# The first batch cut at token 256: four chunks of attention, two MLP units, then the rest, in program order and closed by a fence

## Chip, cores, metric

One core of a Trainium2 chip. The metric is device time in microseconds (us), the median of several executions. All runs quoted were in the same (fast) state. "PE" is TensorE, "DVE" VectorE, "ACT" ScalarE, "POOL" GpSimd, "SP" the engine that issues most DMAs. L-numbers are lines of the kernel that a profile belongs to, so they shift a little from kernel to kernel.

## The reference

```python
# q, k, v: (8 batches, 8 heads, 576 tokens, 64) float32
scores = q @ k.T / 8
ret = scores * where(i >= j, gamma[h] ** (i - j), 0)
attn = ret @ v                                    # (8, 8, 576, 64)
x = attn.transpose(0, 2, 1, 3).reshape(4608, 512)
h = x @ w_in                                      # (512, 2048), float32
g = max(h, 0) + alpha * min(h, 0)                 # alpha per column of h
out = g @ w_out                                   # (4608, 512)
```

## The kernel before

Attention runs by **pairs of heads** (4 pairs per batch, 32 in all) and by **chunks** of 64 tokens (9 per batch): transposes of k and q (`pt`), scores inside chunks (`ps`), states k^T v of chunks (`pu`), their running sums (`su`, copied into `sums`), and values (`pv`), which make x. The MLP runs by **blocks** of 256 tokens (`kb`) and **units** of 2 x 128 columns of h (`i`, 8 per block): 16 matmuls into `ph`, evictions to `g` (ScalarE and VectorE read the finished sums out of `ph`, and only then is `ph` free again), then products `po` with w_out, one unit later. The first two blocks use plain matmuls, the other sixteen a Strassen form (fewer multiplications, more additions). Block 1 needs tokens 256 to 511, block 2 the last 64 tokens of batch 0 and some of batch 1.

The weights come as 32 **pieces** of 512 KB, and each has to be converted.

```python
AHEAD = 5
def fetch(n):                                # SyncE: needs a landing buffer that is free
    ...
        t = free.pop(0)
        nc.sync.dma_start(raw, src)
def load_piece():
    ...
    nc.scalar.activation(a, hi.bitcast(FP32), ACTF.Abs)                    # "wa"
    nc.scalar.activation(lo, lo.bitcast(UINT32), ACTF.Copy, scale=2.0**-29) # "raw" or "w_in"
    nc.vector.tensor_scalar(c.bitcast(FP32), a, HI_MIN, HI_MAX, ALU.max, ALU.min)   # "wc"
    nc.vector.tensor_scalar(c, c, 3, 0x3FFFFFF8, ALU.logical_shift_left, ALU.bitwise_and)
    nc.vector.scalar_tensor_tensor(out=dst, in0=hi, scalar=-0x40000000, in1=c, ...)
    nc.gpsimd.tensor_tensor(out=dst, in0=dst, in1=lo, op=ALU.add)
    free.append(t)                           # the landing buffer is free after GpSimd's add
def load_weights(n):
    for _ in range(n):
        load_piece()
        fetch(npiece[1] + AHEAD)
```

The landing buffers are idle parts of other tiles. The loop that is cut by the change, shortened:

```python
for n in range(1, 4):
    loaded[n] = load_pair(n)                 # q, k, v of a pair, all 576 tokens
    fetch(2 * n)
PIECES = (2, 2, 2, 2, 8, 8, 8, 0)            # pieces converted beside pair n
UNITS = (0, 0, 0, 0, 4, 4, 4, 4)             # plain units beside pair n
for n, (b, c) in enumerate(pairs):
    if 3 < n + 1 < len(pairs):
        loaded[n + 1] = load_pair(n + 1)
    ...
    kT, qT = transposes(n);  load_weights(parts[3])
    at = scores(n, kT, qT);  pop_units(cuts[0]);  load_weights(parts[2])
    states(n, kn, vn);       pop_units(cuts[1]);  load_weights(parts[1])
    values(n, vn, qT, at);   pop_units(cuts[2]);  load_weights(parts[0])
    if c == NPAIR - 1:
        enqueue(b)                           # the first MLP units come after pair 3
```

Nothing fixes the order of instructions of different steps here: the layout of each engine's instruction stream is left to the scheduler.

## Time and profile before

| | before |
|---|---|
| time | 1077.85 us (1076.21 to 1079.26, 4 runs) |
| TensorE busy | 98% of a span of 1076.6 us |
| granted clock, mean | 0.993 |
| first MLP unit runs through | from 66 us |
| last weight piece enters VectorE | 122 us |

Between 80 and 120 us, weights, plain units and pairs 4 to 6 share the engines. Busy time by stretch of the kernel before (columns: PE, PEld, DVE, ACT, POOL busy with counts, granted clock, DMA share, GB/s):

```profile
80.00:90.00 10.00, 10.00 (x75) 7.00 (x68) 9.41 (x15) 5.87 (x16) 9.84 (x10) 1.00 0.85 224
90.00:100.00 10.00, 10.00 (x74) 7.03 (x75) 9.44 (x17) 6.37 (x12) 9.84 (x12) 1.00 0.60 201
100.00:110.00 10.00, 7.72 (x54) 4.89 (x53) 6.08 (x10) 6.13 (x11) 7.26 (x8) 0.93 0.90 280
110.00:120.00 10.00, 10.00 (x94) 6.90 (x93) 9.65 (x19) 7.16 (x17) 6.85 (x8) 0.90 0.61 131
```

Outside 100 to 110 us VectorE is busy 94 to 97% of the time, and TensorE stands still only once, for 2.3 us ahead of 107.6 us.

### The profile page before, as it was taken

How to read it: one execution, taken by the hardware profiler on the slowest of the kernel's cores; microseconds unless marked ns; L12 is line 12 of the kernel's file. 1: busy time of each engine (PE TensorE's matmuls, PEld its weight loads, DVE VectorE, ACT ScalarE, POOL GpSimd, SP SyncE). 2: the span in 40 equal slices, each digit the busy share in tenths (PEclk: the TensorE clock that was granted, in tenths of full speed). 3: DMA queues.
4: the chain of work that ended last, by engine and by line, in shares of the span. 5: the costliest groups of instructions: out<-in, count | busy, mean ns of one | idle time of the engine just before them, and what ended most of it. 6: DMA issues, size and time to landing. Idle time of an engine off the chain costs nothing.

```text
span 1076.6 us, 25072 instructions
## 1 busy us (share of the span) xinstructions
PE 1054.3 (98%) x10321; PEld 927.9 (86%) x10321; DVE 747.0 (69%) x1958; ACT 191.1 (18%) x549; POOL 217.4 (20%) x260
## 2 busy tenths in 40 slices
PE   6899999999999999999999999999999999999998
PEld 5666666899999999999999999999999999999997
DVE  5688612678687777786777777786768676667575
ACT  3666422211110111110100111111111110000000
POOL 4368743411020102010102110201011000100000
PEclk9989999999999999999999999999999999999999
DMA  8857413212222222211112222122222100000000
GB/s 199 242 155 231 100 25 63 76 36 64 45 65 43 56 46 52 47 43 34 35 43 40 60 46 65 35 65 46 65 46 54 24 21 1 21 1 21 1 21 20
DMA packets 212050, 63.25 MB, mean 59 GB/s; under 512 B 201168, under 2 KB 201184, under 8 KB 211936
## 3 DMA queue, kind: packets, MB, share of 16 engines
q1 hardware_dynamic: 209504, 61.04, 24.2%
q8 instruction: 82, 1.34, 0.5%
q10 hardware_dynamic: 2432, 0.60, 0.3%
q14 instruction: 32, 0.26, 0.1%
HBM read 52.17 MB, written 9.44 MB: 57 GB/s over the span
## 4 chain that ended last, share of the span: by engine, by line
PE 93%; DVE 2%; DMA 2%; ACT 1%; issue 1%; POOL 0%; SPq 0%; ACTq 0%; DVEq 0%
PE ph L392 38%; PE po L314 36%; PE ph L350 5%; PE po L329 4%; PE pv L565 3%; PE pv L560 2%; PE ps L523 2%; PE pu L538 2%; PE pt L494 1%; DMA raw<-in_moe_w_in_dram 1%; DMA w_in<-in_moe_w_in_dram 1%; DVE wc L245 1%; DVE wc L248 0%; DMA a<-in_moe_alpha_dram 0%; DMA kn<-in_k_dram 0%
## 5 line engine op out<-in xcount | busy, mean ns | idle before, releaser
L314 PE MATMUL po<-w_out,g 128*128 128x256 f32 x1792 | 407.8, 379 | 0.0
L314 PEld LDWEIGHTS po<-w_out,g 128*128 128x128 f32 x1792 | 330.8, 190 | 39.7
L403 DVE TENSOR_TENSOR g<-ph,g 128x256 f32<-128x256 f32 (+1 forms) x512 | 187.4, 387 | 180.2 <-PE ph L392 103.6
L392 PE MATMUL ph<-xb,w_in 128*128 128x128 f32 x2048 | 277.7, 279 | 0.0
L392 PEld LDWEIGHTS ph<-xb,w_in 128*128 128x128 f32 x2048 | 253.1, 192 | 8.2 <-issue 0.5
L392 PE MATMUL ph<-xt,w_in 128*128 128x128 f32 x1536 | 213.3, 275 | 0.0
L392 PEld LDWEIGHTS ph<-xt,w_in 128*128 128x128 f32 x1536 | 192.1, 192 | 0.0
L414 DVE TENSOR_TENSOR g<-g 128x128 f32<-128x128 f32 x512 | 144.0, 322 | 7.8
L398 ACT COPY g<-ph 128x128 f32<-128x128 f32 x128 | 34.0, 265 | 479.5 <-PE ph L392 472.0
L462 POOL TENSOR_TENSOR vn<-vn,th 128x512 f32<-128x512 f32 (+1 forms) x60 | 42.0, 718 | 380.9 <-DMA vn<-in_v_dram 380.8
L408 DVE SCALAR_TENSOR_TENSOR g<-g 128x512 f32<-128x512 f32 x128 | 94.3, 737 | 3.9
L406 DVE TENSOR_SCALAR g<-g,alpha 128x256 f32<-128x256 f32 x256 | 88.7, 388 | 4.5
L350 PE MATMUL ph<-xb,w_in 128*128 128x256 f32 x256 | 65.3, 404 | 2.8 <-DVE g L359 2.3
L375 POOL TENSOR_TENSOR xt<-xb,xt 128x256 f32<-128x256 f32 x32 | 25.1, 786 | 175.2 <-ACT xb L451 174.6
L350 PEld LDWEIGHTS ph<-xb,w_in 128*128 128x128 f32 x256 | 48.9, 198 | 13.2 <-issue 4.7
L329 PE MATMUL po<-w_out,g 128*128 128x512 f32 x128 | 57.8, 593 | 1.1 <-DVE g L359 1.1
L451 ACT COPY xb<-pv 128x128 f32<-128x128 f32 (+1 forms) x176 | 29.6, 269 | 129.1 <-PE pv L565 129.1
L329 PEld LDWEIGHTS po<-w_out,g 128*128 128x128 f32 x128 | 24.2, 190 | 24.5 <-issue 22.0
L552 ACT COPY sums<-su 64x512 f32<-64x512 f32 x64 | 39.5, 617 | 29.4 <-DVE su L549 28.6
L527 DVE SCALAR_TENSOR_TENSOR at<-ps,th,mask 128x320 f32<-128x320 f32 x64 | 32.4, 544 | 15.9 <-PE ps L523 15.9
L506 DVE STREAM_TRANSPOSE qT<-qn 128x576 f32<-128x576 f32 x24 | 18.7, 778 | 33.8 <-PE pv L565 30.5
L565 PE MATMUL pv<-qT,sums 128*64 128x64 f32 x1024 | 41.2, 235 | 0.2 <-ACT sums L552 0.2
(90 smaller groups left out, 686.8 us busy)
## 6 DMA issues: line engine op xcount, KB each, us to landing
out_dram<-osb SPq DMA_DIRECT2D x36, 256.0 KB, 2.3
kn<-in_k_dram SPq DMA_DIRECT2D x60, 128.0 KB, 2.9
vn<-in_v_dram SPq DMA_DIRECT2D x60, 128.0 KB, 2.7
kx<-in_k_dram SPq DMA_DIRECT2D x96, 72.0 KB, 2.4
qn<-in_q_dram SPq DMA_DIRECT2D x96, 72.0 KB, 2.5
raw<-in_moe_w_in_dram SPq DMA_DIRECT2D x11, 512.0 KB, 4.3
raw<-in_moe_w_out_dram SPq DMA_DIRECT2D x11, 512.0 KB, 4.6
w_in<-in_moe_w_in_dram SPq DMA_DIRECT2D x5, 512.0 KB, 6.0
```

What stands on the lines that cost most here:

```text
L314: nc.tensor.matmul(acc[kb][n // 2][:, n % 2, :], g[:, x, :], w_out[i][:, y, :], start=(i == 0 and n % 2 == 0), stop=(i == NU - 1 and (n % ...
L329: nc.tensor.matmul(acc[kb][m], g[:, 2 * x + m], w_out[i][:, 2 * x:2 * x + 2].rearrange("p x f -> p (x f)"), start=(i == 0 and x == 0), sto ...
L350: nc.tensor.matmul(ph[:, x], w_in[i // UST][:, cc // 2 * 2 + x, cc % 2, f0:f0 + P], xb[kb][:, cc], start=(cc == 0), stop=(cc == NCC - 1))
L392: nc.tensor.matmul(ph[m][:, o], w_in[i // UST][:, l, cc, f0:f0 + P], r[:, cc], start=(n in (0, 3) and cc == 0), stop=(n in (2, 6) and cc = ...
L398: nc.scalar.copy(g[:, 7], ph[0][:, 2])
L403: nc.vector.tensor_tensor(out=o, in0=x0, in1=x1, op=ALU.add)
L406: nc.vector.tensor_scalar(g[:, 4 + 2 * m:6 + 2 * m], g[:, 2 * m:2 * m + 2], 0.0, alpha[:, fc:fc + 1], ALU.min, ALU.mult)
L408: nc.vector.scalar_tensor_tensor(out=g[:, 0:4].rearrange("p x t -> p (x t)"), in0=g[:, 0:4].rearrange("p x t -> p (x t)"), scalar=0.0, in1 ...
L414: nc.vector.tensor_tensor(out=g[:, o, :], in0=g[:, x0, :], in1=g[:, x1, :], op=op)
L462: nc.gpsimd.tensor_tensor(out=t[0:rows, m], in0=t[0:rows, m], in1=th[0:rows, x, None, 2 * c:2 * c + 2, None].to_broadcast([rows, n, 2, D]) ...
L552: nc.scalar.copy(sm[half(h2), :, h2], su[half(h2)])
L565: nc.tensor.matmul(pv[j % 2][half(h2), j // 2], sm[:, j - 1, h2], qT[:, chunk(j)], start=False, stop=(j >= NJ - 2), skip_group_check=True)
```

## The change

Intent: TensorE has to wait for x of block 0 only as long as four of the nine chunks take. So batch 0 is split at token 256: loads and attention of four chunks for all pairs (part 0), block 0's first two units, the other five chunks (part 1), block 1's first two units, all in the order in which the program writes it (`manual_schedule`), then a fence in the layout (`no_sync_barrier`), after which the rest is laid out as before. The diff, cut to its core:

```diff
-    loaded = {0: load_pair(0)}
+    CUT = TB // C                                  # 4 chunks
+    PARTS = ((0, CUT), (CUT, NJ))
+    ... # k, q, v of a part, all heads, in unused space of w_out
+    load_part(0)
...
-            queue.extend((kb, i) for i in range(NU) for kb in PLAIN)
+            queue.extend((kb, i) for i in range(UST, NU) for kb in PLAIN)
...
     # transposes, scores, states, values take (pair, first chunk, last chunk);
     # states of part 0 are kept, and carried into part 1
...
+    with tc.manual_schedule():
+        fetch(2 * NST)
+        load_part(1)
+        ...
+        for f in (0, 1):
+            scale_part(0, 1 + f, f)
+        steps(0, "t0 t1 s0 u0 s1 u1 v0 t2 t3")
+        load_weights(1)
+        steps(0, "v1 s2 u2")
+        load_weights(1)
+        steps(0, "s3 u3 v2")
+        load_weights(1)
+        steps(0, "v3")
+        alphas()
+        load_weights(3)
+        mlp_unit(0, 0)
+        load_weights(1)
+        mlp_unit(0, 1)
+        load_weights(1)
+        mlp_out()
+        for f in (0, 1):
+            scale_part(1, 1 + f, f)
+        steps(1, "t0 t1 s0 u0 s1 v0 u1 t2 s2 v1 u2 t3")
+        load_weights(1)
+        steps(1, "s3 v2 u3")
+        load_weights(1)
+        steps(1, "v3")
+        load_weights(1)
+        mlp_unit(1, 0)
+        load_weights(2)
+        mlp_unit(1, 1)
+        fetch(4 * NST)
+        loaded = {n: load_pair(n) for n in (NPAIR, NPAIR + 1)}
+    tc.no_sync_barrier()
+    enqueue(0)
-    for n in range(1, 4):
-        loaded[n] = load_pair(n)
-        fetch(2 * n)
-    PIECES = (2, 2, 2, 2, 8, 8, 8, 0)
-    UNITS = (0, 0, 0, 0, 4, 4, 4, 4)
+    PIECES = {NPAIR: 9, NPAIR + 1: 8, NPAIR + 2: 2}
```

## The prediction

> **What bounds the kernel now.** I read the page's busy shares and slices first, then the busy time by stretch, the chain that ended last, the waits, and the groups by form.
>
> ```profile
> PE 1054.3 (98%) x10321; PEld 927.9 (86%) x10321; DVE 747.0 (69%) x1958; ACT 191.1 (18%) x549; POOL 217.4 (20%) x260
> PE   6899999999999999999999999999999999999998
> PEld 5666666899999999999999999999999999999997
> ```
>
> TensorE is the bound in every slice but the first few. So the change, which touches only the first 180 us or so, can win only what TensorE wastes there, and matmul busy time does not show that waste: the same transposes are in the chain twice, at two speeds. The busy time by stretch shows where little is done:
>
> ```profile
> 0.00:10.00 10.00, 1.67 (x7) 1.21 (x8) 5.43 (x36) 1.98 (x3) 6.21 (x18) 1.00 0.89 171
> 10.00:20.00 10.00, 9.24 (x138) 7.58 (x138) 5.33 (x11) 5.12 (x11) 3.98 (x6) 1.00 0.80 199
> 20.00:30.00 10.00, 8.42 (x104) 7.13 (x101) 7.18 (x13) 5.27 (x14) 4.69 (x6) 1.00 0.90 229
> 30.00:40.00 10.00, 10.00 (x126) 8.19 (x126) 4.00 (x8) 3.02 (x7) 3.43 (x5) 1.00 1.02 355
> 40.00:50.00 10.00, 8.54 (x175) 6.90 (x174) 7.29 (x15) 9.62 (x26) 2.60 (x2) 0.86 0.59 133
> 50.00:60.00 10.00, 7.71 (x82) 5.95 (x82) 9.09 (x16) 7.19 (x19) 7.12 (x8) 0.67 0.99 259
> ```
>
> (columns: PE, PEld, DVE, ACT, POOL busy, granted clock, DMA share, GB/s). I therefore keep a ledger of TensorE work at full speed, with prices from the chain where it runs without a pause:
>
> ```profile
> 116.39 0.73 PE pv L560 x36
> 117.12 1.08 PE pv L565 x32
> 118.20 3.65 PE ph L350 x16
> 121.85 3.43 PE po L329 x8
> 125.28 0.64 PE pt L494 x5
> ```
>
> and from the same view 0.75 us for 40 score matmuls and, from the timeline, 0.69 us (0.62 of it without the drain) for 32 state matmuls. One pair of heads is 2 x 0.64 + 0.75 + 0.62 + 0.73 + 1.08 = 4.5 us. One plain unit is 16 x 0.216 + 3.43 = 6.9 us (I take 3.46 for the 16 because the 3.65 includes one drain).
>
> Ledger of before, by counting those instructions: at 66 us, where the first unit's 16 matmuls begin to run undisturbed, four pairs and parts of the fifth are done, 25 us of work, so 41 us are lost. At 125.3 us, when the weights are all but converted (the last piece enters VectorE at 121.9 us), six pairs and 8 x 3.46 + 7 x 3.43 of units are done: 26.8 + 51.7 = 78.5 us, so 46.5 us are lost. After that TensorE runs on. **The prize is those 46 us at most, 4.3% of the time.**
>
> Why they are lost: the first MLP unit needs x of tokens 0 to 255 from all four pairs, and a pair computes all 576 tokens. The waits of TensorE and VectorE up to 60 us are for loads and for single small steps:
>
> ```profile
> PE pt L494 <- DMA kn<-in_k_dram: 8.3, 2, 5.0
> PE pv L560 <- DVE su L549: 3.8, 3, 2.3
> DVE wc L245 <- ACT wa L240: 10.3, 4, 7.5
> DVE su L544 <- ACT su L543: 6.0, 2, 4.9
> ```
>
> The first full unit ends near 72 us although 12 weight pieces are through VectorE by 66 us, and four of those complete w_in's first quarter: x came last, not the weights.
>
> **What the Trainium skill says.** "TensorE: Matmul & The Clock Gate", Part 1, has TensorE at half its clock until it was busy for some 3.4 us. This case agrees in effect: five transposes take 1.38 us at 5 and 9.7 us but 0.64 us at 125 us. The granted clock column shows 1.00 in those cold stretches, so I go by durations. The same page's advice to avoid idle gaps over about 3 us matters here, because the change makes two short phases with pauses in between. "Perfetto Trace Analysis", Identifying the Most-Contended Engine, says matmul busy share is a poor measure; here 9.24 of 10 us "busy" hold only 3 to 4 us of full-speed work. "DMA: Bandwidth & Descriptors", Specifications, puts the line-rate limit at runs of 512 B; q, k and v move in 256 B runs before and after, and the trace has 171 to 229 GB/s while they dominate against 355 GB/s in 30 to 40 us.
>
> **The change, part by part.**
> - Loads. Removed from the front: q, k, v of whole pairs (3.5 MB, pair by pair, mixed with weights). Added: 4/9 of them for all heads first (1.57 MB, six DMAs), then eight weight pieces (4.2 MB), then the other 5/9 (2.0 MB). At about 230 GB/s after 2.5 us latency: first part at 9 us, the eighth piece near 27 us, the rest near 36 us. Later pieces are fetched five ahead, so loads should not bind.
> - Scaling on GpSimd: four operations of 128x512 for part 0 and six for part 1, at 1.04 us each: 4.2 and 6.2 us. Before, it was spread; now part 1's six stand in program order behind the eighth piece's add.
> - Attention. The same matmuls: a pair's 4.5 us becomes 1.9 (four chunks) + 2.6 (five). What grows is the number of small VectorE and ScalarE steps: one more carry, two more copies into the block sums per pair, and shorter operations at nearly the same fixed cost. About 1 us per pair of ScalarE and 0.7 of VectorE, 7 us in all, on engines with room.
> - Part 0 timeline (estimate). Transposes from 7 us, q scaled 8 to 9 us, at the cold rate four pairs at roughly 4 us each: x of block 0 near 26 us.
> - Weights: three pieces go in between, each 3 x 0.69 = 2.1 us of VectorE and 1.29 of GpSimd. The fourth lands on w_in at 26 + 0.9 (alpha) + 2.1 + 1.3 = 30 us. **Unit (0,0) starts at 30 us**, where before the ledger's first whole unit started at 59 to 66 us. Lost so far: 30 - 4 x 1.9 = 22 us.
> - Units (0,0), (0,1): 13.8 us, plus 1.7 us for the cold clock, plus 2 us because the last product needs piece 8, which stands behind both units' VectorE work in program order: end at about 47 us, lost 26.
> - Part 1: q scaled on GpSimd 44 to 47, v to 50 us; then four pairs. A pair's chain from states to values is 0.3 (ACT) + 1.1 (four VectorE steps) + 1.1 (four ScalarE copies) + some 0.6 of signals, 3 us; with two pairs interleaved I get about 4.5 us a pair, so x of block 1 at about 67 us against 10.4 us of work: lost 35.
> - Units (1,0), (1,1): 67 to 77 us and on, one product left pending. At 74 us the ledger gives 17.9 + 13.8 + 6.9 = 38.6, lost 35.4. Before at 72.2 us: lost 41.3. Gain here: **6 us**.
> - After the fence 12 plain units and 19 pieces (9, 8, 2) remain, where before 16 units ran while 24 pieces came. Before lost another 5.2 us between 72 and 125 us: 2.3 + 1.1 us of waits for g at 107 us, when VectorE was full of pieces (9.4 of 10 us between 80 and 100 us), and the slower clock that followed (0.91). After, stage 1 is asked for at 77 us with 13 pieces through, stage 2 at about 110 us with 10 more to do (17 us of VectorE in 33). I count 3 us lost instead of 5: **2 us more**.
>
> The fence costs no instruction and no wait; it only limits the order in which the program is laid out. Sum: 6 + 2 = 8 to 9 us, so 1078.2 - 9 = **1069 us**.
>
> **The rivals.**
> 1. *The wait moves into part 1.* In strict program order a late step on one engine holds everything behind it. If a part-1 pair takes 6.5 us instead of 4.5, 8 us vanish and the time is about 1077. For it: the chains of waits before are just such steps (DVE su <- ACT su 6.0 us), and GpSimd's scaling starts late. Against: TensorE is warm there and loads are in.
> 2. *Weights become the bound.* Block 0 wants its pieces 30 us earlier. Eight pieces are 17 us of VectorE and land by 27 us, but if the conversions interleaved with part 0 delay it, or stage 1 is late after the fence, the gain is 2 to 4 us: 1075. VectorE's 9.4 of 10 us at 80 to 100 us speak for it.
> 3. *The front fills better than I think.* If block 0 starts at 26 us and part 1 hides beside it more, 28 us are lost in the front instead of 35: about 1061. For it: nothing in the trace keeps part 0's pairs at 4 us each but the cold clock.
> 4. *The order after the fence is worse.* The layout of the remaining program is made afresh; a hole of 20 us would be needed to matter at 2%. Nothing points to it.
>
> **Range and chances.** Rivals 1 and 2 bring it to 1075 to 1079, rival 3 to 1060; runs spread by 3 us. I say 1069, 8 in 10 between 1059 and 1078. Faster by over 2% means under 1056.7, a gain of 21.5 of the 46 lost us while 22 are spent before any unit could start: 0.05. Slower by over 2%: 0.02. Within 2%: 0.93.
>
> **What would show it.** Unit (0,0)'s first matmul at 28 to 33 us; block 0's last product at 45 to 49; unit (1,0) at 64 to 70; TensorE waits in 47 to 67 us for ScalarE block sums or GpSimd's scaling; ledger loss at 125 us of 36 to 40 instead of 46.5; the stretch from 200 us to the end as long as before within 3 us. It is wrong if unit (0,0) waits for weights beyond 36 us, if part 1 takes over 25 us, or if the later stretch changes by over 5 us.

## The result and the profile after

| | before | after |
|---|---|---|
| time | 1077.85 us (1076.21 to 1079.26) | 1112.44 us (1111.44 to 1113.73) |
| profiled span | 1076.6 us | 1109.7 us |
| TensorE busy | 98% | 96% |
| granted clock | 0.993 | 0.983 |

Ratio 1.0322, 95% interval 1.0303 to 1.0341: slower by 34.6 us, where 9 us faster was predicted. Ratios here are the mean time of one kernel's fast runs over that of the other's of the same rounds, so not quite the ratio of the medians quoted. The rounds of the experiments ran on different chips; runs of different rounds are therefore compared through their ratios.

**Where it went.** The ledger of the prediction, taken further: at time t, the TensorE instructions that have started are counted and priced at full speed, and t minus that sum is what was lost. (Later work is priced from the undisturbed stretch: 0.111 and 0.216 us for a Strassen matmul of `ph` and `po`.)

| lost by, us | 50 | 66 | 82 | 100 | 118 | 140 | 160 | 200 | 1065 |
|---|---|---|---|---|---|---|---|---|---|
| before | 32.8 | 41.0 | 41.5 | 42.2 | 46.4 | 46.9 | 47.7 | 48.7 | 63.3 |
| after | 32.2 | 39.9 | 50.3 | 57.1 | 66.0 | 75.0 | 79.0 | 81.0 | 96.5 |
| after - before | -0.6 | -1.1 | +8.8 | +14.9 | +19.6 | +28.1 | +31.3 | +32.3 | +33.2 |

The last column agrees with the spans (33.1 us apart). So by 66 us, in the middle of part 1, next to nothing has been gained; at its end, 82 us, the change is 9 us behind; the next 120 us cost 23 us more; and from 200 us on the two kernels are alike.

**Front and part 1.** TensorE's timeline after (start, length, instruction, and in brackets the idle time before it and what ended it):

```profile
32.41 2.08 PE L369 MATMUL ph<-xb,w_in 128*128 128x256 f32 x4
36.14 1.22 PE L369 MATMUL ph<-xb,w_in 128*128 128x256 f32 x2 [1.65 <-POOL w_in L268]
38.46 8.56 PE L369 MATMUL ph<-xb,w_in 128*128 128x256 f32 x26 [1.10 <-POOL w_in L268]
...
52.57 2.84 PE L345 MATMUL po<-w_out,g 128*128 128x512 f32 x6 [1.26 <-POOL w_out L268]
55.25 2.30 PE L530 MATMUL pt<-ident,w_out 128*128 128x128 f32 x12
...
74.14 0.58 PE L563 MATMUL ps<-qT,kT 64*64 64x64 f32 x24 [2.06 <-ACT qT L534]
...
82.05 2.50 PE L369 MATMUL ph<-xb,w_in 128*128 128x256 f32 x5
```

Block 0 begins at 32.4 us but waits for converted pieces and runs freely only from 38.5. Its last product ends at 55.4. Part 1 takes 55.25 to 82.05, **27 us for 10.4 us of work**. TensorE's waits in it (55 to 82 us; who waits for whom, then us in total, times, longest):

```profile
PE ps L563 <- ACT qT L534: 3.8, 2, 2.1
PE pv L621 <- DVE w_out L602: 1.6, 1, 1.6
PE pu L583 <- DVE at L567: 1.4, 2, 0.8
```

With two smaller ones they sum to 7.8 us, under half of the 16 us lost. In the rest of part 1 TensorE is busy, but slowly: 19.1 us for matmuls that the ledger prices at 10.4, at a mean granted clock of 0.67. Busy time by stretch, after:

```profile
60.00:70.00 10.00, 7.63 (x130) 5.97 (x130) 3.33 (x11) 3.71 (x13) 0.00 (x0) 0.55 0.01 2
70.00:80.00 10.00, 5.59 (x108) 4.27 (x107) 4.95 (x13) 5.08 (x18) 1.28 (x1) 0.67 0.10 9
80.00:90.00 10.00, 10.00 (x70) 8.62 (x71) 5.82 (x10) 6.54 (x16) 2.57 (x2) 0.76 0.20 71
90.00:100.00 10.00, 5.36 (x17) 2.62 (x15) 6.06 (x10) 3.20 (x6) 2.58 (x2) 0.93 0.68 163
100.00:110.00 10.00, 10.00 (x68) 6.59 (x68) 6.37 (x10) 5.62 (x12) 10.00 (x11) 0.73 0.67 156
110.00:120.00 10.00, 4.89 (x43) 3.25 (x42) 3.55 (x6) 3.54 (x7) 6.86 (x9) 0.78 0.59 145
```

In 60 to 80 us no engine is over 80% busy, and TensorE's share is that of a slowed clock; the DMAs move 2 and 9 GB/s. SyncE's and GpSimd's waits in part 1 say why the transfers stopped:

```profile
SPq L244 <- POOL w_in L268: 25.5, 1, 25.5
```

```profile
POOL w_in L268 <- DVE w_in L266: 18.6, 1, 18.6
```

SyncE has the next fetch ready for 25.5 us but no landing buffer: that comes free with GpSimd's add, which waits 18.6 us for VectorE's step on the piece, which stands in the order behind part 1's attention steps. So no weight piece enters VectorE between 49 and 75 us, and the reserve of landed pieces is not refilled.

**After the fence.** The last 24 of the 32 pieces enter VectorE one per 4.0 us (75 to 168 us); before, the last 21 came one per 2.8 us (65 to 122 us). Lines of the timeline of all engines, after, around the longest stop:

```profile
105.00 0.68 ACT L256 ACTIVATE wa<-raw 128x512 f32<-128x512 f32 x1
...
106.04 0.57 SPq L244 DMA_DIRECT2D raw<-in_moe_w_in_dram  x1
...
111.00 0.68 ACT L258 ACTIVATE raw<-raw 128x512 int32<-128x512 uint32 x1 [5.32 <-DMA raw<-in_moe_w_in_dram]
...
114.48 0.67 ACT L258 ACTIVATE raw<-raw 128x512 int32<-128x512 uint32 x1 [2.80 <-DMA raw<-in_moe_w_in_dram]
115.05 0.58 ACT L372 ACTIVATE g<-ph 128x512 f32<-128x512 f32 x1
...
117.17 2.05 PE L369 MATMUL ph<-xb,w_in 128*128 128x256 f32 x4 [5.11 <-DVE g L378]
```

This is how such a stop is read. TensorE waited 5.1 us "for VectorE's g", but VectorE had waited for ScalarE's eviction of `ph`, whose matmuls had been done by 108.0 us. The eviction came at 115.05 because two conversion steps stood ahead of it in ScalarE's stream, and their pieces had not landed; the transfer that ended the first wait was asked for only at 106.04, when ScalarE had been ready for it since 105.7. From 93.3 us until then SyncE had been issuing the loads of pairs 4 and 5, one after another. The Trainium skill's page "PSUM — Partial Sum Buffer", Engine vs sequencer instructions, calls the queues of ScalarE, VectorE and GpSimd strictly first-in-first-out; the trace agrees: a finished `ph` waited 7 us behind a step it has nothing to do with. ScalarE's waits for landing pieces between 82 and 170 us, after and then before:

```profile
ACT raw L258 <- DMA raw<-in_moe_w_out_dram: 11.3, 3, 6.3
ACT raw L258 <- DMA raw<-in_moe_w_in_dram: 9.9, 3, 5.3
ACT w_in L258 <- DMA w_in<-in_moe_w_out_dram: 2.7, 1, 2.7
```

```profile
ACT raw L242 <- DMA raw<-in_moe_w_in_dram: 2.9, 1, 2.9
ACT w_in L242 <- DMA w_in<-in_moe_w_in_dram: 2.3, 2, 1.4
ACT raw L242 <- DMA raw<-in_moe_w_out_dram: 2.2, 3, 0.8
```

(24 us against 7 us in these lines.) Another stop is 4.6 us of TensorE at 94 to 98.7 us for k of the next pair, whose loads stand behind `fetch` in SyncE's queue.

Of the 30 us that TensorE loses between 82 and 170 us, 17 are waits and 12 are matmuls that run longer than at full speed (granted clock 0.89 on average); before, the same stretch has 2.3 us of waits and 4 of slow running (0.98). So a wait is not the whole cost of a stop. And GpSimd is busy all of 100 to 110 us (10.00; before, 9.84 in 80 to 100), so for that stretch the trace alone does not rule out its capacity.

### The profile page after: what moved, and what is told of

It is laid out like the page before. It is cut to its first block, busy times and chain, and to the rows that moved or that the text cites. A ratio compares the mean times of both kernels' runs of the same rounds, so it can differ in the third digit from the quotient of the medians.

```text
span 1109.7 us, 25062 instructions
## 1 busy us (share of the span) xinstructions
PE 1059.9 (96%) x10321; PEld 928.7 (84%) x10321; DVE 752.2 (68%) x1974; ACT 194.2 (18%) x569; POOL 217.0 (20%) x254
## 3 DMA queue, kind: packets, MB, share of 16 engines
q1 hardware_dynamic: 209488, 61.11, 23.5%
## 4 chain that ended last, share of the span: by engine, by line
PE 85%; DMA 1%; DVE 1%; POOL 1%; ACT 0%; issue 0%; SPq 0%; DVEq 0%; POOLq 0%; ACTq 0%
PE ph L411 37%; PE po L330 35%; PE pv L627 3%; PE po L345 2%; PE ph L369 2%; PE ps L563 2%; PE pv L621 2%; PE pu L583 1%; DMA raw<-in_moe_w_out_dram 1%; DMA vn<-in_v_dram 0%; PE pt L530 0%; DVE wc L264 0%; POOL w_in L268 0%; POOL w_in L274 0%; POOL w_out L274 0%
## 5 line engine op out<-in xcount | busy, mean ns | idle before, releaser
L411 PEld LDWEIGHTS ph<-xb,w_in 128*128 128x128 f32 x2048 | 253.1, 192 | 8.2 <-DVE g L433 0.2
L482 POOL TENSOR_TENSOR vn<-vn,th 128x512 f32<-128x512 f32 (+1 forms) x56 | 39.2, 719 | 371.1 <-DMA vn<-in_v_dram 369.4
L369 PE MATMUL ph<-xb,w_in 128*128 128x256 f32 x256 | 71.8, 435 | 9.1 <-DVE g L378 6.3
L369 PEld LDWEIGHTS ph<-xb,w_in 128*128 128x128 f32 x256 | 53.2, 217 | 20.0 <-ACT wa L256 5.2
L567 DVE SCALAR_TENSOR_TENSOR at<-ps,th,mask 128x320 f32<-128x320 f32 (+2 forms) x72 | 33.6, 507 | 28.0 <-PE ps L563 27.9
L378 DVE SCALAR_TENSOR_TENSOR g<-g,nalpha,ph 128x256 f32<-128x256 f32 x32 | 13.9, 476 | 43.0 <-ACT ph L374 43.0
L627 PEld LDWEIGHTS pv<-qT,sums 128*64 128x64 f32 x1000 | 35.7, 149 | 8.2 <-ACT sums L609 5.6
```

Source lines behind the costliest of these rows:

```text
L369: nc.tensor.matmul(ph[:, x], w_in[i // UST][:, cc // 2 * 2 + x, cc % 2, f0:f0 + P], xb[kb][:, cc], start=(cc == 0), stop=(cc == NCC - 1))
L411: nc.tensor.matmul(ph[m][:, o], w_in[i // UST][:, l, cc, f0:f0 + P], r[:, cc], start=(n in (0, 3) and cc == 0), stop=(n in (2, 6) and cc = ...
L482: nc.gpsimd.tensor_tensor(out=t[0:rows, m], in0=t[0:rows, m], in1=th[0:rows, x, None, 2 * c:2 * c + 2, None].to_broadcast([rows, n, 2, D]) ...
L567: nc.vector.scalar_tensor_tensor(out=at[h2][:, 0:nm], in0=ps[h2], scalar=th[:, 3, h:h + 1], in1=mask[:, None, :].to_broadcast([P, nm, C]), ...
L627: nc.tensor.matmul(pv[j % 2][half(h2), j // 2], sm[:, at0 + j - first, h2], qT[:, chunk(j)], start=False, stop=(j >= nj - 2), skip_group_c ...
```

## The experiments

The candidate causes, by name: (order) strict order makes every late step hold everything behind it, above all in part 1; (fence) the fence makes a worse layout after it; (loads) the next pairs' loads are asked for too late, behind fetches that wait for buffers; (clock) TensorE's slow clock lengthens part 1; (buffers) too few landing buffers. The expectations use letters of their own: A is the hole in the weight stream between 49 and 75 us, which was my first theory, A' its empty landing buffers, B the split itself, C a part 1 made slow by program order, D the late loads. Ratios are to the kernel before of the same rounds; the change itself is 1.0322. One hundredth of the time is 10.8 us.

### One part of the change undone

**e1_free**, no order, the fence stays; **e2_nofence**, order without fence; **e3_neither**.

```diff
-    with tc.manual_schedule():          # e1_free, e3_neither
+    with ExitStack():
-    tc.no_sync_barrier()                # e2_nofence, e3_neither
```

> The changed kernel with the program-order region removed, so the compiler's scheduler orders all engines again; the split at token 256 and the fence stay. Theory A (a hole in the weight stream: no piece enters VectorE between 49.0 and 74.8 us, because program order puts only three pieces into part 1, and everything later starves): the scheduler pulls pieces forward, the ninth piece enters before 60 us and the time falls by 15 to 30 us, to 1082-1097. Theory B (the split itself costs: more small steps and a cold TensorE clock): still above 1105. Theory C (program order makes part 1 slow by 7 us, weights are not the matter): 1103-1107.

> The changed kernel without the fence; program order inside the region stays. Theory A with the fence as its lid (pieces of stage 1 and 2, and the units of batch 0, may not move up beside part 1): conversions fill 50 to 75 us, time falls by 10 to 25 us. Theory A without the fence's part (the five-ahead ring and the order on each engine keep the pieces back): within 4 us of 1112. Theory B: within 4 us of 1112.

> The changed kernel with both the program-order region and the fence removed; the split, the loads' place in the queue and the share of pieces stay. So far: order removed 1092, fence removed 1099. If the two lose time in one and the same place (stage 1 to 3 pieces held back), removing both gives little more than the order alone: 1086-1092. If they are separate losses they add: 1078-1084.

Measured: 1092.22 us, 1.0165 [1.0147, 1.0183]; 1099.19 us, 1.0228 [1.0213, 1.0243]; 1086.79 us, 1.0101 [1.0068, 1.0134]. Taking the order out gives back about 17 us, the fence about 10, both together 24. Both (order) and (fence) hold in part, and neither is enough. Without order the front does what the prediction hoped for: in e1 block 0's first matmul starts at 22.6 us and 26.7 us are lost at 50 us, 6 less than before. With strict order that gain was gone by then: VectorE's stream has a weight piece ahead of the scores of a pair and waits 4.25 us, until 20.1 us, for ScalarE's step on it, and TensorE's waits for `at` (the scaled scores) up to 50 us sum to 7.6 us. In e1 the first piece enters VectorE at 12.6 us.

**e5_loads**, order and fence kept, the loads of the next two pairs asked for at the start.

```diff
         load_part(1)
+        loaded = {n: load_pair(n) for n in (NPAIR, NPAIR + 1)}
...
         fetch(4 * NST)
-        loaded = {n: load_pair(n) for n in (NPAIR, NPAIR + 1)}
```

> The changed kernel with the loads of pairs 4 and 5 issued right after part 1's loads instead of behind the fetches of pieces 8 to 15 in the same queue. Theory D (these loads stand behind fetches that wait for free slots: they start at 93.3 us and TensorE waits 4.6 us for k at 98.7 us): the wait vanishes and the time falls by 4 to 8 us. If A alone holds, weights bound that stretch anyway and the time stays within 3 us, or gets worse by up to 4 us because 2.4 MB then delay piece 8.

Measured: 1100.53 us, 1.0243 [1.0222, 1.0264]. (loads) is worth 8 to 9 us; the wait for k is gone from TensorE's list, and the fetches after 93 us no longer stand behind the issue of these loads. The two were not separated.

**e8_all_undone**, no order, no fence, early loads: the split alone.

> The split alone: no program order, no fence, loads of pairs 4 and 5 early. Theory B (the split itself, with its smaller steps, its part-1 chains and its few pieces in front, costs against before): stays above 1080. Theory that ordering devices are the whole loss and the early unit is worth what I predicted: 1065-1072. With the measured single effects (17, 10, 9 us) partly overlapping I expect 1080-1086.

Measured: 1084.24 us, 1.0074 [1.0041, 1.0106]. The three removals give 17 + 10 + 9 us one by one but only 27 together, so they overlap. Even the split alone doesn't gain: it is 5.9 us ahead of before at 66 us (35.1 lost against 41.0), 2.4 behind at 90 us and 6.1 behind at 200 us.

**e6_before_fence**, the kernel before with nothing added but the fence ahead of pair 4.

```diff
+        if n == NPAIR:
+            tc.no_sync_barrier()
```

> The kernel before with one fence and nothing else: placed ahead of pair 4, where the changed kernel has its own. If a fence costs because it keeps pieces and units from moving up beside small steps: slower than before by 8 to 20 us. If it costs only together with the region: within 4 us of before.

Measured: 1086.64 us, 1.0104 [1.0075, 1.0134]. A fence without any instruction costs 11 us in a kernel that is otherwise untouched. Its ledger departs from before in one place (lost at 100 us 44.6, at 118 us 54.8), and ScalarE's and TensorE's timeline there shows the same picture as after:

```profile
100.92 0.65 ACT L242 ACTIVATE raw<-raw 128x512 int32<-128x512 uint32 x1 [5.86 <-POOL w_out L252]
...
104.45 0.65 ACT L242 ACTIVATE raw<-raw 128x512 int32<-128x512 uint32 x1 [2.33 <-DMA raw<-in_moe_w_in_dram]
105.00 0.58 ACT L353 ACTIVATE g<-ph 128x512 f32<-128x512 f32 x1
```

```profile
107.12 6.66 PE L350 MATMUL ph<-xb,w_in 128*128 128x256 f32 x16 [6.59 <-DVE g L359]
```

Two conversion steps wait, the eviction stands behind them, TensorE stops for 6.6 us, and the 16 matmuls after it take 6.66 us where 3.5 are full speed.

### More weights in part 1, more buffers, a warm clock

**e4_pieces**: six pieces instead of three between part 1's steps, 8 and 8 after the fence.

```diff
-        steps(1, "t0 t1 s0 u0 s1 v0 u1 t2 s2 v1 u2 t3")
-        load_weights(1)
-        steps(1, "s3 v2 u3")
+        steps(1, "t0 t1 s0 u0")
+        load_weights(1)
+        steps(1, "s1 v0 u1")
+        load_weights(1)
+        ...                              # and three more
-    PIECES = {NPAIR: 9, NPAIR + 1: 8, NPAIR + 2: 2}
+    PIECES = {NPAIR: 8, NPAIR + 1: 8}
```

> The changed kernel with six weight pieces instead of three placed in part 1, one after every second or third step, so that 16 pieces instead of 13 stand before the fence (and 8, 8 after it); nothing else. Theory A: the ninth piece enters VectorE near 60 us instead of 74.8, the last one 10 to 20 us earlier than 167.8, and the time falls by 8 to 20 us, although part 1 grows by 3 to 6 us. Theories B and C: part 1 only gets longer, time 1112-1120.

Measured: 1114.65 us, 1.0371 [1.0355, 1.0386], slightly worse. The ninth piece enters VectorE at 61.4 us instead of 74.8, the last one at 159.2 instead of 167.8, and no time is won, where my first theory (A, the hole in the weights) had 8 to 20 us. e1 fell into A's range, with the ninth piece at 43.3 us; but e8 and e17 below keep holes of 24 and 21 us and lose little, so the hole by itself is not what costs. Without order and fence (**e13_free_pieces**) the same pieces are neutral:

> The split with no order and no fence (as in the run that gave 1086.8), but six weight pieces instead of three given to part 1. With the scheduler free, more pieces early should keep the stream running between 50 and 70 us: 1076-1084 if the stream's place is what is left, 1085-1090 if the split's own chains are. In program order the same edit had made it 2 to 5 us slower.

Measured: 1087.02 us, 1.0085 [1.0064, 1.0106], as e3_neither.

**e7_ring**: two landing buffers kept longer, seven pieces ahead instead of five.

```diff
-    AHEAD = 5
+    AHEAD = 7
...                                      # and fetch stops when no buffer is free
-    gone = {"x3": UST * NST, "x4": UST * NST, 1: 2 * UST * NST}
+    gone = {"x3": 2 * UST * NST, "x4": 2 * UST * NST, 1: 2 * UST * NST}
```

> The changed kernel with order and fence as they are, but two more landing buffers for pieces 8 to 15 (two x buffers kept for weights until piece 16 instead of piece 8) and fetches seven ahead instead of five. Theory A' (the fetch ring is empty after the hole: the DMA queue waits 34 us for GpSimd to free a buffer between 60 and 90 us, moves 5 GB/s from 60 to 80 us, and after 93 us ScalarE waits 25 us for pieces to land, with evictions of MLP units behind it): time falls by 6 to 14 us. If the conversions themselves are late for their place in the order and not for their data: within 3 us.

Measured: 1117.04 us, 1.0385 [1.0356, 1.0414]. (buffers) falls in this form: more buffers did not help, the time rather grew, which neither expectation allowed. They end at piece 16, so that more of them for the later pieces would help is not excluded.

**e15_warm**: 24 dummy matmuls of 128x256 (48 matmul instructions in the trace), three ahead of each score and value step of part 1.

> The changed kernel with three matmuls of 128x256 more, whose result nobody reads, ahead of each score and value step of part 1: 24 in all, 10 us of TensorE work at full clock, in order in front of waits. In part 1 TensorE runs at a granted clock of 0.55 to 0.67 in 60 to 80 us. If the cold clock is a large share of part 1's 27 us and of the cold units after it, part 1 does not grow and the time falls by 2 to 6 us; if part 1 is bound by ScalarE's and VectorE's steps, the clock is a symptom and the time grows by 0 to 6 us.

Measured: 1111.28 us, 1.031 [1.0288, 1.0332], the change's own time. Busy time by stretch:

```profile
60.00:70.00 10.00, 9.05 (x145) 6.73 (x145) 3.25 (x11) 4.42 (x17) 0.00 (x0) 1.00 0.01 3
70.00:80.00 10.00, 9.16 (x150) 6.84 (x148) 4.43 (x11) 3.90 (x12) 0.37 (x1) 1.00 0.01 2
```

The granted clock is now 1.00 where it was 0.55 and 0.67, and part 1 takes 28.7 us instead of 26.8 (lost at 80 us 49.6, without the dummies 49.3, where the dummies count as lost). This does not refute (clock). Part 1's own matmuls now take 14.6 us instead of 19.1, and TensorE's waits are 2.3 us instead of 7.8; the dummies, 10.4 us of work at full speed, stand in order in front of the real matmuls and used up what both gained. So the slow clock costs part 1's matmuls some 4.5 us. What a full clock would save without the dummies no run shows: the waits for ScalarE and VectorE could grow again.

### The transfers taken away

**e11_no_dma**, the change, and **e12_before_no_dma**, the kernel before, without the weights' transfers (wrong results; the conversion runs on a constant).

```diff
-            nc.sync.dma_start(raw, src)
-        lo, hi = raw[:, :, :, 0], raw[:, :, :, 1]
+        lo = raw[:, :, :, 0]
+        hi = ident[:, 0:1].bitcast(INT32)[:, :, None].to_broadcast([P, 2, HM])
...
-        nc.scalar.activation(lo, lo.bitcast(UINT32), ACTF.Copy, scale=2.0 ** -29)
+        nc.scalar.activation(lo, hi.bitcast(UINT32), ACTF.Copy, scale=2.0 ** -29)
```

> Wrong results on purpose: the changed kernel without the transfers of the weights; each conversion reads a constant of the same shape in place of the landed piece, every conversion step, buffer and place in the order is kept. It takes away the landing times, and the waits of fetches for free buffers in the DMA queue with the loads behind them. If the loss is weights that land late with ScalarE's evictions stuck behind them in order: 1078-1090 (20 to 30 us gone). If it is the order of the conversions themselves and part 1's length: 1098-1110.

> The same removal in the kernel before, also wrong on purpose, as the control: what landing times cost there. The ledger of before has 5 us lost between 72 and 125 us and 41 before that, so I expect 1060-1072. The difference between this and the run above is what the change costs with weights always there; I expect +15 to +22 us from part 1 and its place in the order.

Measured: 1098.03 us, 1.0185 [1.0164, 1.0207]; 1076.93 us, 0.9987 [0.9952, 1.0022]. Before loses nothing to the transfers on balance, where 6 to 18 us were expected: its ledger is 5 us ahead at 66 us (36.0 lost against 41.0), but 3 behind at 100. The change loses 14 us to them. But 21 us of its loss remain without a single transfer of weights, so late landing is not the whole mechanism. The waits of ScalarE and VectorE in e11 between 82 and 170 us show what stays:

```profile
ACT w_in L258 <- POOL w_out L268: 9.8, 4, 5.5
```

```profile
DVE su L597 <- ACT su L593: 16.0, 3, 9.6
```

ScalarE's conversion step now waits for GpSimd's add on an earlier piece, which still uses that buffer, and behind ScalarE stands a copy that VectorE needs. The chain is a ring: SyncE needs the buffer from GpSimd, ScalarE the piece, VectorE ScalarE's result, GpSimd VectorE's, and each of the three works its stream in order, with attention and evictions in between.

### The ring cut

**e17_no_act**, the change, and **e18_before_no_act**, the kernel before, with a piece converted by VectorE alone; ScalarE's two steps and GpSimd's add are gone (wrong results). All transfers stay.

```diff
-        nc.scalar.activation(a, hi.bitcast(FP32), ACTF.Abs)
-        nc.scalar.activation(lo, lo.bitcast(UINT32), ACTF.Copy, scale=2.0 ** -29)
-        nc.vector.tensor_scalar(c.bitcast(FP32), a, HI_MIN, HI_MAX, ALU.max, ALU.min)
+        nc.vector.tensor_scalar(c.bitcast(FP32), hi.bitcast(FP32), HI_MIN, HI_MAX, ALU.max, ALU.min)
-        nc.gpsimd.tensor_tensor(out=dst, in0=dst, in1=lo, op=ALU.add)
```

> Changed kernel with the conversion of a weight piece reduced to its three VectorE steps, reading the landing buffer directly; ScalarE's two steps and GpSimd's add are gone (wrong result on purpose). Theory: after the fence ScalarE, in order, stands before steps on weights that have not landed, with MLP evictions behind them; then the gap to its control e18_before_no_act shrinks from 34 to under 18 us (after about 1090, control about 1074). Rival: the coupling is through VectorE's order or through the transfers themselves, which remain; then the gap stays at 27 us or more.

> Control: the kernel before with the same reduction of the conversion (wrong result on purpose). Expected 1070 to 1078: it lost only some 5 us after 66 us, so there is little to win.

Measured: 1080.99 us, 1.0036 [1.0021, 1.0051]; 1073.49 us, 0.9965 [0.995, 0.998]. **The gap falls from 34.6 to 7.5 us**, more than expected, with order, fence and late loads all in place. The ledger of e17 has 26.0 us lost at 50 us (after: 32.2), 39.9 at 82 (50.3) and 51.4 at 200 (81.0). The control gains only 4 us from the same edit, so the work that it saves is worth little where nothing is held up. The 7.5 us left arise between 82 and 100 us (lost 39.9 to 48.0; in e18 about 41 to 41.5). Half of what e17 loses there is waits, and TensorE's only large one is for the late k; the other half is slow running (granted clock 0.81):

```profile
PE pt L523 <- DMA kn<-in_k_dram: 3.6, 1, 3.6
```

**e20_no_scalar**: only ScalarE's two steps out (GpSimd adds the high words instead, wrong). **e21_no_pool**: only GpSimd's add out (the low words are dropped).

> Changed kernel, only ScalarE's two conversion steps removed; GpSimd's add stays (on the high words, wrong on purpose). If ScalarE's order is the coupling, near e17_no_act's 1.004 of before, at most 1.012. If it is GpSimd that frees the landing buffers late and fills them late, 1.02 or more.

> Changed kernel, only GpSimd's add removed; ScalarE's two steps stay (wrong on purpose). If ScalarE's order is the coupling, 1.02 or more; if GpSimd is, 1.012 or less.

Measured: 1092.48 us, 1.0163 [1.0132, 1.0194]; 1096.35 us, 1.0199 [1.017, 1.0228]. So my sharper form of the theory, "ScalarE's order carries it", fails: it demanded 1.012 at most for e20. Its rival, GpSimd alone, demanded the same of e21 and fails too. Each engine's part alone gives back 13 to 17 us of the 35, both together 31 (these compare with the kernel before as it is; e20 and e21 have no control of their own, and against e18 both together give back 27). So the cost lies in the chain over both and not in one of them. Whether it is the steps' place in the two in-order streams or only the time that they add to a piece's way to a free buffer, these runs do not separate.

### Attempts at a version that wins

**e16_mid_loads**: no order, no fence, pair 4's loads after block 0's last product, pair 5's at the old place. **e19_mid_loads_pieces**: the same with six pieces in part 1.

> Changed kernel without order and fence, the loads of pair 4 asked for after block 0's last product and those of pair 5 at the old place. e3_neither (loads late) gave 1086.8, e8_all_undone (all early) 1084.2. If the loads' place is what still costs there, about 1080; if it is part 1 itself, 1084 to 1087.

> The same as e16_mid_loads with six weight pieces in part 1 instead of three. If weights in part 1 are worth something once the order is free, 2 to 5 us less than e16_mid_loads; if not, the same within 1.5 us, as e13_free_pieces was to e3_neither. A candidate to beat the kernel before (1076): I give it one chance in five.

Measured: 1087.27 us, 1.0094 [1.0075, 1.0113]; 1088.73 us, 1.0109 [1.0094, 1.0124]. Neither the place of the loads nor more pieces removes what the split alone costs. No version with the split beat the kernel before.

## Why the prediction was wrong, step by step

| step of the prediction | predicted | measured |
|---|---|---|
| unit (0,0) starts | 30 us, 22 lost | 32.4 us, 24.9 lost |
| block 0's last product | 47 us, 26 lost | 55.4 us, 33.9 lost at 55.2 |
| part 1 | 20 us | 27 us |
| lost at 74 us | 35.4 (before 41.3) | 45.2 |
| lost at 125 us | 36 to 40 | 68.1 |
| from the start of units (1,0), (1,1) to 200 us | 2 us better than before | 23.5 us worse (50.3 to 81.0 lost; before 41.5 to 48.7) |
| after 200 us | unchanged within 3 us | 15.5 us lost, before 14.6 |

**The largest miss: "I count 3 us lost instead of 5" after the fence.** I priced that stretch by capacity (17 us of VectorE in 33 us, where the nine pieces in question make 19) although the profile of before had VectorE 94% busy there. The capacity was right and beside the point: VectorE is only 36 to 64% busy after, in 90 to 120 us. What I did not price is that a piece passes through three in-order engines and frees its landing buffer at the end. Once the reserve of landed pieces is spent, each of them has conversion steps standing in front of attention steps and evictions. The trace shows it at 105 to 117 us, e6 reproduces such a stop without any of the change's instructions, and with ScalarE's and GpSimd's steps gone (e17) the loss from 82 to 200 us falls from 30.7 to 11.5 us.

**"The fence costs no instruction and no wait" was half true and led wrong.** No instruction, yes; but 11 us by itself (e6) and 10 us within the change (e2 against after). Rival 4 named this ("the order after the fence is worse"), and I dismissed it with "nothing points to it". In the kernel before, the tuned layout was itself something the time rested on, and the fence discarded it.

**Part 1, rival 1.** The mechanism was named (a late step in strict order holds everything behind it), and 6.5 us per pair was its price; 27 us over four pairs is 6.7. I chose the lower figure because TensorE would be warm there. It was not (clock 0.55 and 0.67): the matmuls took 8.7 us more than their price and the waits 7.8 us, and e15 shows the same matmuls 4.5 us shorter at a clock of 1.00. But my price for rival 1, 8 us and a time of 1077, left out what part 1 does to the weights: a hole of 26 us in their supply (which by itself does not explain the loss: e4, e8, e17).

**Block 0, rival 2.** Unit (0,0) waited for conversions as rival 2 had it: it ran freely at 38.5, with pieces interleaved with part 0 delaying both. The block ended with 8 us more lost than predicted: 3 from the late start, and 9 instead of 4 during the block, which are 4.0 us of stalls (1.65 + 1.10 + 1.26) and 5.0 us of matmuls below full speed, for which the prediction had 1.7. (Its remark that the granted clock shows 1.00 in the cold first stretches is no measurement: the trace's clock records begin at 40 us before and at 44 us after.)

**Rival 3** (the front fills better) came true only without strict order: block 0's first matmul starts at 22.6 us (e1), and the front is 6 us ahead of before. It is spent again by 90 us (e8).

**The loads.** "Loads should not bind" failed: k of the next pair came 4.6 us late, behind fetches that waited for buffers, and then held up the next fetches; asking for these loads early gave 8 to 9 us (e5).

**The range** followed from adding these as independent small terms. Several of them share one chain (taken out one by one they give 17 + 10 + 9 us, together 27), so they came together; 0.02 for slower was far too sure.

**What stays open.** e8, e16 and e19 still lose 8 to 12 us with the split alone; the ledger of e8 puts the loss at 66 to 90 us (the end of part 1, whose last values end at 72 us, block 1's units and pair 4) and at 118 to 140 us, but no run isolates a cause. What the slow clock costs by itself stays open too (e15). That e17 and e8 end at nearly the same ratio to their controls (1.007) suggests a common remainder; that is argued, not shown. Nor did a run show a repair: conversion by one engine with right results was not built.

## What to carry to other kernels

Before adding strict order or a fence to a tuned kernel, look for chains that pass through several in-order engines and end by freeing the buffer that starts them: here they did not show in busy shares, and they stopped TensorE once their reserve was empty. Test a fence alone on the old kernel first; it is one line and showed a third of this loss. When TensorE waits "for" an eviction, look at what stood ahead of that eviction in its engine's stream, and when that thing's transfer was asked for. And a probe that adds work on the path it tests, like the dummy matmuls, hides what it wins: count its own time before reading the total.

## What the Trainium skill lacked or had wrong

- No page has the price of a pure layout fence: it adds no instruction, and cost 11 us (1.0104) in the kernel before.
- "PSUM — Partial Sum Buffer", Engine vs sequencer instructions, has the in-order queues right, but not what follows for a buffer ring over three of them: a finished `ph` waited 7 us behind a step on an unlanded piece, and taking ScalarE's and GpSimd's steps out of the ring gave back 27 us against its control.
- "TensorE: Matmul & The Clock Gate", Part 1, advises to keep TensorE from idle gaps, but not what it costs to fill them. Here 24 dummy matmuls raised the granted clock from 0.55 and 0.67 to 1.00 in 60 to 80 us and made part 1's matmuls 4.5 us shorter, but are 10.4 us of work themselves, and the time stayed (1.031 against 1.0322 of before).
